# Cosine attention followed by a low-rank mixer and an MLP: mixer tiles that wait in DRAM, another order of the score bursts, and a fifth pair of tiles with seven products in both layers

## The chip, the cores and the metric

The kernel runs on one core of a Trainium2 chip. The metric is the device time of one execution in microseconds; the median of several runs is compared. The engines are TensorE (PE in the profile), VectorE (DVE), ScalarE (ACT), GpSimd (POOL) and SyncE (SP), and 16 DMA engines that serve the queues of POOL and SP.

## The reference, cut to what matters

There are 8 batches, 12 heads, 448 positions and a head width of 64. Each head is normalised, scored, put through a softmax and multiplied with its values. The heads side by side are a matrix of 448 x 768 for each batch. A low-rank map over the positions (rank 32) is added to it, and a two-layer MLP (768 to 3072 to 768) with a residual follows.

```
q_n = q / (norm(q) + 1e-6);  k_n = k / (norm(k) + 1e-6)
attn = softmax(q_n @ k_n.T / tau)
x = heads_side_by_side(attn @ v)                 # 8 x 448 x 768
u = x + (x.transpose(0, 2, 1) @ U @ V).transpose(0, 2, 1)
out = u + relu(u @ w_ch1) @ w_ch2
```

All matmuls of the kernel take bf16 operands and add up in fp32.

## The kernel before, in words

**A program that plans itself.** Each piece of work is an `Op` with an engine, an expected duration, the ops that it depends on (`deps`), the buffers that it takes (`acq`) and gives back (`rel`). Buffers are `Slot`s of a `Ring`; the eight PSUM banks are shared by several `BankRing`s. `Plan.run` goes through time with these durations, gives every engine its next op, and so fixes the order of instructions on each engine. On PE the ops stand in streams with a fixed order of preference: the values of attention (`pe_av`), the mixer (`pe_z0`, `pe_a`), the scores (`pe_sc`) and, last, the MLP (`pe_mlp`), which fills what the others leave. POOL has one stream (`pool_q`) in the order in which the code writes it. ACT, DVE and SP take what is ready by priority. On the chip each engine works through its list in order and waits on semaphores where an input is not there.

**Attention of a batch** (`att`, `scores`, `values`). POOL loads q and k in thirds of four heads, and v. `stats` and `norm` compute the norms on ACT and DVE and scale q and k; SP turns them with DMA transposes into `qkT` (for the first two batches PE does it). A slot of scores is one pair of heads against up to 128 keys: two matmuls of 448 columns, one for each head, which use one half of the rows of the array each. 448 keys make three slots of 128 keys and a rest of 64; the rests of two pairs share a slot of four matmuls that use one quarter of the array each. From batch 2 on `groups_of` puts the three slots of rests of a batch first and then the 18 others, and cuts the list into bursts of three, seven a batch. ACT takes the exp of each slot (L727). `values` (L754) multiplies with v; DVE divides by the sum of the softmax and writes X.

**The mixer** (`stage0`). Two batches (896 positions) make seven tiles of 128 positions, so that tile 3 holds the end of the even batch and the start of the odd one. A is X projected on U; one product with V for each tile and half of the columns, and an add of X on DVE (L918, L920, L923), give the tile u. Tile 3 is made in the odd batch, from both batches' A and X. The tiles u lie in eight SBUF buffers (`r_u`) until the MLP has added its residual.

**The MLP.** There are 28 tiles. The plan's MLP work is done in this order:
- Five plain units (`mlp`) of 3, 4, 3, 3 and 3 tiles. `columns_of` turns their u by DMA transposes into uT (one buffer). The first layer is 24 blocks of six matmuls over all columns of the unit (384 or 512; L1273), each followed by a relu on ACT or DVE. The second is 24 matmuls of 384 columns for each tile and half of the output (L1309), an add of the residual on DVE and stores on SP.
- Two pairs of tiles with seven products in the second layer alone (`mlp_seven` without `up`): the 2 x 2 block product (two tiles by two halves of the output, two halves of the inner width) is made of seven products instead of eight, 84 matmuls of 384 columns (L1196) instead of 96. The first layer is plain, 288 matmuls of 256 columns for both tiles (L1167).
- Four pairs with seven products in both layers (`up_seven`): the first layer is 252 matmuls of 128 columns (L1066).

The seven products need sums of blocks of the weights and of the data. The sums of the second layer's weights are made by `seven_weights`, those of the first by `seven_rows`, which puts them into attention's buffers and therefore waits for the last batch. The sums of the data after the relu are made by `sums_of` (L1148 to L1151): in the pairs with seven products in both layers its last difference is done by POOL for the first two of three groups and by DVE for the third. In each pair, product 1 of the second layer is copied by ACT (L1217), POOL adds u to the copy three times (L1219), and DVE adds the banks of the other products to these (L1212). PE's order there is product 1, 4, 6, 5, 7, 2, 3; the sum that DVE makes after product 6 goes into the bank to which product 7 adds.

**What ties attention to the MLP.** The bursts of batches 2 to 7 have extra dependencies on matmuls of the MLP: batch 2's on the first layer of unit 1, batches 3 to 5's on places in the second layers of units 1 to 3 (`SPOTS`), and batches 6 and 7's on places in unit 4 and in the first two pairs. The first burst of a batch also waits for the mixer's products of the batch before.

Of the kernel before, what the change touches and what calls it, by code (L numbers as in the profile page):

```python
# [101 lines left out]
class Plan:  # L102
# [53 lines left out]
    def run(self):  # L156
# [22 lines left out]
        while left:  # L179
# [6 lines left out]
            while progress:  # L186
                progress = False
                for e in self.ENGINES:
# [81 lines left out]
def kernel(  # L270
# [30 lines left out]
    SPOTS = {8: [(6,)] * 7 + [()], 6: [(5, 17), (10,), (6,), (6,), (6,), (6,)]}  # L301
# [47 lines left out]
    r_u = fixed_ring([u_t[:, i, :] for i in range(8)])  # L349
# [55 lines left out]
    r_low = bank_ring([(5,), (4,), (3,), (2,), (1,), (0,)], 2)  # L405
# [327 lines left out]
    def values(b, p, X):  # L733
# [39 lines left out]
        for hh in range(2):  # L773
# [21 lines left out]
    prev, first_v, made = {}, {}, {}  # L795
# [51 lines left out]
    def stage0(b, X, muls):  # L847
# [39 lines left out]
        us = [Slot(r_u, 2 if b == 0 else 6 if by_pe else 3) for t in tiles]  # L887
# [7 lines left out]
        for z, (c0, c1) in enumerate(cols):  # L895
            for i, t in enumerate(tiles):
# [3 lines left out]
                elif t == 3:  # L900
                    parts = [(prev["A"], PAD + 128 * t), (A, 0)]
# [24 lines left out]
                rel = [mm, X] + ([prev["X"]] if t == 3 else [])  # L926
# [3 lines left out]
                adds[z, i] = plan.add(Op("DVE", dve_t(c1 - c0) * (2 if t == 3 else 1), add,  # L930
# [104 lines left out]
    def up_seven(tiles, relu, tops, ready, left, made_by, x_free):  # L1035
# [61 lines left out]
        for k in (1, 6, 2, 7, 5, 3, 4):  # L1097
            for g in range(len(gs)):
# [25 lines left out]
                else:  # L1124
# [3 lines left out]
                    sums_of(gs[g], relu, ready, [x["r11"]], [x["r12"]], [x["r21"]], [x["r22"]], "POOL" if g < 2 else "DVE")  # L1128
# [26 lines left out]
    def mlp_seven(tiles, right, made_by, up=None, after=()):  # L1155
# [58 lines left out]
        def tile_of(s):  # L1214
# [5 lines left out]
            out=y_.tile, in0=s1.tile, in1=u.tile[:, c0:c0 + CH]), deps=[cp], acq=[y_], rel=[s1, u]), pool_q)  # L1220
            for y_, u, c0 in ((y12, u1, CH), (y22, u2, CH), (y21, u2, 0))]
        if up is not None:
# [13 lines left out]
            x11 = dve(bank(tile_of(o11), lambda: u1.tile[:, 0:CH], a), [p2], [o11], [a, u1])  # L1236
# [8 lines left out]
        x11 = dve(bank(tile_of(o11), lambda: u1.tile[:, 0:CH], a), [p2], [o11], [a, u1])  # L1245
# [14 lines left out]
    def mlp(b, tiles, us, uT, ut):  # L1260
# [42 lines left out]
        for group in groups:  # L1303
# [12 lines left out]
            for (i, t, c0, c1), mm in zip(group, mms):  # L1316
# [5 lines left out]
                    deps=[last[mm]] + got.get((b, "u"), []), acq=[O], rel=[mm, us[i]], prio=1))  # L1322
# [68 lines left out]
    def groups_of(b):  # L1391
# [87 lines left out]
    UNITS = [[(0, 0), (0, 1), (0, 2)], [(0, 3), (0, 4), (0, 5), (0, 6)], [(1, 0), (1, 1), (1, 2)],  # L1479
             [(1, 3), (1, 4), (1, 5)], [(1, 6), (2, 0), (2, 1)]]  # L1480
    for b, tiles in enumerate(UNITS):
        mlp(b, tiles, *(state[b] if b < PE_BATCHES else columns_of(tiles)))
    rest = [(z, t) for z in range(2, 4) for t in range(7)][2:]
    seven = seven_weights(last_down[len(UNITS) - 1],
                          [o for p in range(NPAIR) for o in got[B - 1, p, "qkT"][1]],
                          [last_av[B - 2, p] for p in range(NPAIR)])
    PURE = 4
    hosts = []
    for n in range(0, len(rest), 2):
        if n // 2 == len(rest) // 2 - PURE:  # L1490
            up = seven_rows([hosts[-1][0][-1]], [last_av[B - 1, p] for p in range(NPAIR)])
            held = list(stores)
            up = *up, [o for t in range(7) for o in made[3, t][1]]
        late = n // 2 >= len(rest) // 2 - PURE
        hosts.append(mlp_seven(rest[n:n + 2], *seven, *((up, held) if late else ())))
    (t0, l0), (t1, l1) = hosts[:2]
    t4, d4 = anchors[4]
# [50 lines left out]
```

## Time and profile before

| | us |
|---|---|
| median of 3 runs | 565.98 (565.66 to 566.13) |
| the profiled execution | 565.53 |
| its span, first to last instruction | 563.8 |
| PE busy | 552.9 (98%) |
| DVE busy | 395.4 (70%) |
| ACT busy | 282.1 (50%) |
| POOL busy | 135.2 (24%) |
| SP's DMA queue | 23.98 MB, 21.5% of 16 engines |
| POOL's DMA queue | 25.73 MB, 40.9% of 16 engines |

The span is the time from the first to the last instruction in one profiled execution; some 1.7 us of the execution's time lie around it. The busy time of PE is the union of its matmuls' spans, and these overlap: a matmul of 384 columns is shown with 326 ns, and the next one starts 162 ns after it. What a matmul costs in a stream is the distance from start to start, which is the length of a piece in the chain of waits over its number of matmuls. In the windows by stage each row gives the stretch, its length, then busy time and number of instructions for PE, PE's weight loads, DVE, ACT and POOL, the granted clock of TensorE, the busy share of the DMA engines and what they moved in GB/s. The share can exceed 1[...]. In the timeline a bracket holds the idle time before an instruction and what ended it.

The last score matmuls run at 411 us and the last products with v at 416 us; the four pairs with seven products in both layers fill the time from 445.6 us on.

### The profile page before, as it was taken

The page shows a single profiled execution, that of the slowest core. Times are in us where ns is not written, and L with a number is a line of the kernel's source. Part 1 is how long each engine was busy: PE and PEld are TensorE (multiplying, and loading weights), DVE is VectorE, ACT ScalarE, POOL GpSimd, SP SyncE. Part 2 cuts the span into 40 slices and gives each one's busy share as a digit, 9 for nine tenths or more (in the row PEclk, how much of TensorE's full clock was granted, in tenths as well). Part 3 has the DMA queues.
Part 4 walks back from the last instruction along what each step waited for, and adds up shares of the span by engine and source line. Part 5 has one row for each costly group of instructions (what it writes and reads, how often), then busy time and mean ns, then how long its engine had stood idle before and what let it go on. Part 6 is the DMA issues. An engine that isn't in the chain of part 4 may idle for free.

```text
span 563.8 us, 13573 instructions
## 1 busy us (share of the span) xinstructions
PE 552.9 (98%) x5639; PEld 361.0 (64%) x5639; DVE 395.4 (70%) x901; ACT 282.1 (50%) x466; POOL 135.2 (24%) x170
## 2 busy tenths in 40 slices
PE   8999999999999999999999999999999999999996
PEld 6565566544565565566555655677677787878783
DVE  8989969987674786478337743489468685858582
ACT  7876645668525671666554665336343131414140
POOL 8526242060041105002310300000102013131313
PEclk9899999999999999999999999999999999999999
DMA  9999999795769649596958534310211111112201
GB/s 149 201 208 135 209 199 151 120 111 80 121 77 152 96 68 104 111 114 55 103 107 131 56 30 102 73 29 16 31 44 29 57 30 57 30 57 30 57 3 56
DMA packets 132670, 50.58 MB, mean 90 GB/s; under 512 B 97760, under 2 KB 132608, under 8 KB 132608
## 3 DMA queue, kind: packets, MB, share of 16 engines
q0 software_dynamic: 72352, 25.73, 40.9%
q1 hardware_dynamic: 60256, 23.98, 21.5%
q8 instruction: 44, 0.72, 0.6%
q14 instruction: 18, 0.15, 0.1%
HBM read 52.02 MB, written 11.01 MB: 112 GB/s over the span
## 4 chain that ended last, share of the span: by engine, by line
PE 84%; DVE 9%; issue 2%; POOL 1%; ACT 1%; POOLq 1%; DMA 1%; DVEq 0%
PE bank L1309 23%; PE bank L1273 23%; PE bank L1196 9%; PE bank L754 8%; PE bank L709 6%; PE bank L1167 6%; PE bank L1066 5%; DVE relu L1088 4%; PE bank L909 2%; DVE v_nat L1088 1%; PE bank L502 1%; POOL relu L1151 1%; ACT attn L722 1%; PE bank L859 1%; POOLq L1543 1%
## 5 line engine op out<-in xcount | busy, mean ns | idle before, releaser
L727 ACT ACTIVATE attn<-bank 128x896 bf16<-128x896 f32 (+1 forms) x163 | 139.0, 917 | 72.9 <-PE bank L709 72.4
L1309 PE MATMUL bank<-w_sb,relu 128*128 128x384 bf16 x768 | 136.7, 326 | 0.0
L1273 PE MATMUL bank<-uT,w_sb 128*128 128x384 bf16 (+1 forms) x720 | 135.7, 337 | 0.0
L1309 PEld LDWEIGHTS <-relu 128*128 128x128 bf16 x768 | 70.9, 98 | 52.7 <-issue 10.3
L1273 PEld LDWEIGHTS <-w_sb 128*128 128x128 bf16 x720 | 67.1, 98 | 54.8 <-issue 7.4
L1196 PEld LDWEIGHTS <-relu 128*128 128x128 bf16 x504 | 48.6, 98 | 34.8 <-issue 4.1
L580 DVE TENSOR_REDUCE ss<-sq_all 112x8 f32<-112x512 bf16 x96 | 61.9, 672 | 3.8 <-ACT sq_all L572 3.4
L1296 ACT ACTIVATE relu<-bank 128x384 bf16<-128x384 f32 (+1 forms) x80 | 40.8, 511 | 46.4 <-PE bank L1273 46.0
L648 DVE TENSOR_TENSOR qk_all<-qk_all,inv 112x512 bf16<-112x512 bf16 x93 | 60.7, 680 | 0.1
L754 PEld LDWEIGHTS <-attn 128*128 128x128 bf16 (+1 forms) x1536 | 54.5, 98 | 9.2 <-issue 3.1
L754 PE MATMUL bank<-v_nat,attn 128*128 128x65 bf16 (+1 forms) x1536 | 57.5, 193 | 0.5 <-DVE qkT L1338 0.3
L1196 PE MATMUL bank<-w_sb,relu 128*128 128x384 bf16 x288 | 50.1, 326 | 2.1 <-DVE qkT L1212 1.0
L524 POOL DMA_DIRECT2D qk_all<-in_q_dram x24 | 17.4, 727 | 136.9 <-ACT attn L727 50.2
L547 POOL DMA_DIRECT2D v_nat<-in_v_dram x42 | 31.1, 746 | 72.7 <-PE bank L754 41.7
L709 PE MATMUL bank<-qkT 64*128 64x448 bf16 (+1 forms) x384 | 47.3, 357 | 1.2 <-ACT qkT L1336 0.6
L1320 DVE TENSOR_TENSOR O_sb<-bank,u_nat 128x384 f32<-128x384 f32 x32 | 17.7, 555 | 34.2 <-PE bank L1309 34.0
L785 DVE TENSOR_TENSOR X_sb<-bank,rd 128x256 bf16<-128x256 f32 x96 | 38.9, 416 | 1.6 <-DVE rd L783 0.2
L1151 POOL TENSOR_TENSOR relu<-relu 128x512 bf16<-128x512 bf16 x8 | 17.2, 2170 | 88.2 <-ACT qkT L1217 42.7
L783 DVE RECIPROCAL rd<-bank 128x4 f32<-128x4 f32 x96 | 16.5, 176 | 27.7 <-PE bank L754 26.8
L1298 DVE TENSOR_SCALAR relu<-bank 128x384 bf16<-128x384 f32 (+1 forms) x40 | 23.3, 584 | 16.9 <-PE bank L1273 16.4
L572 ACT ACTIVATE sq_all<-qk_all 112x512 bf16<-112x512 bf16 x53 | 31.1, 630 | 7.6 <-DVE ss L580 7.6
L1066 PE MATMUL bank<-uT,w_sb 128*128 128x128 bf16 x576 | 34.1, 219 | 0.0
(116 smaller groups left out, 643.6 us busy)
## 6 DMA issues: line engine op xcount, KB each, us to landing
qk_all<-in_q_dram POOLq DMA_DIRECT2D x23, 224.0 KB, 5.4
qk_all<-in_k_dram POOLq DMA_DIRECT2D x23, 224.0 KB, 6.3
w_sb<-in_moe_w_ch_dram POOLq DMA_DIRECT2D x4, 1152.0 KB, 18.8
w_sb<-in_moe_w_ch_dram POOLq DMA_DIRECT2D x8, 576.0 KB, 15.8
out_dram<-O_sb SPq DMA_DIRECT2D x13, 168.0 KB, 2.3
v_nat<-in_v_dram POOLq DMA_DIRECT2D x11, 168.0 KB, 8.7
out_dram<-O_sb SPq DMA_DIRECT2D x12, 144.0 KB, 2.8
out_dram<-O_sb SPq DMA_DIRECT2D x12, 120.0 KB, 2.0
```

The lines of the kernel that those rows point to most:

```text
L580: lambda i=i, a0=a0, a1=a1, sq=sq: nc.vector.reduce_sum(ss.tile[:, i, a0:a1, :].rearrange("p h c -> p (h c)"), sq.tile[:, 0:a1 - a0, :].re ...
L648: nc.vector.tensor_mul(dst, src, sc)
L709: nc.tensor.matmul(out=out, lhsT=qkT.tile.rearrange("p b s -> p (b s)")[r, n0:n0 + w], rhs=qkT.tile[r, SC:2 * SC, :].rearrange("p c s -> p ...
L727: exps.append(plan.add(Op("ACT", act_t(2 * S, 0.08), lambda sc=sc, c=c, attn=attn: nc.scalar.activation(out=attn.tile[:, :, off:off + S] i ...
L754: nc.tensor.matmul(out=av.tile[:, t, 0:D + 1], lhsT=tail.tile[:, hh, 128 * t:128 * (t + 1)] if tail and j == SC - 1 else (attn if j < SC - ...
L785: muls.append(plan.add(Op("DVE", dve_t(256), lambda av=av, rd=rd, h=h: nc.vector.tensor_mul(X.tile[:, :, h * D:(h + 1) * D], av.tile[:, :, ...
L1066: o = plan.add(Op("PE", pe_t(128), lambda i=i, j=j, jj=jj: nc.tensor.matmul(out=mm.tile[:, 128 * jj:128 * jj + 128], lhsT=left[k](i, j), r ...
L1167: o = plan.add(Op("PE", pe_t(256), lambda j=j, e=e, cc=cc, mm=mm: nc.tensor.matmul(out=mm.tile[:, 256 * e:256 * e + 256], lhsT=w1_sb[:, cc ...
L1196: o = plan.add(Op("PE", pe_t(CH), lambda j=j: nc.tensor.matmul(out=mm.tile[:, 0:CH], lhsT=left[k](j), rhs=right[k](j), start=(first and j ...
L1273: o = plan.add(Op("PE", pe_t(n), lambda cc=cc: nc.tensor.matmul(out=mm.tile[:, 0:n], lhsT=w1_sb[:, cc, f * 128:(f + 1) * 128], rhs=uT.tile ...
L1296: nc.scalar.activation(out=relu.tile[:, f, 0:n], in_=mm.tile[:, 0:n], func=AF.Relu)
L1309: nc.tensor.matmul(out=mm.tile[:, 0:c1 - c0], lhsT=relu.tile[:, f, i * 128:(i + 1) * 128], rhs=w2_t[:, f, c0:c1], start=(f == 0), stop=(f ...
```

## The change

- **u tiles in DRAM.** For batches 2 to 7 each finished tile u is written by SP into a DRAM tile (`kept`). `columns_of` takes the DMA transposes from there, and reads the tile back into SBUF for the residual (`u.back`). The eight SBUF buffers become two rings of four (`r_us` for making, `r_ur` for the residual).
- **Tile 3** is made in two halves, the first 64 rows in the even batch, the others in the odd one.
- **Score bursts.** The dependencies on the MLP's matmuls go. In batches 3 to 7 burst 0 waits for the last product with v of the batch before, burst 1 for that batch's mixer products, bursts 3 and up for the products with v of pair k - 3 of its own batch.
- **Rests of keys.** The three slots of 64-key rests are spread over the batch (`LAST`): each is sorted to the end of a burst of other slots.
- **Units.** The plain units are of 3, 4, 3 and 4 tiles; two pairs have seven products in the second layer alone, five pairs in both.
- `sums_of` in `up_seven` is on DVE for all three groups. `r_low` may hold four banks. From batch 2 on the first product with v also takes the X buffer. A count of needed buffers in `Plan.run` is corrected.

```diff
@@ Plan.run
-                            room = [x.ring.free_at(new[:n].count(x.ring)) for n, x in enumerate(new)]
+                            room = [x.ring.free_at([y.ring for y in new[:n]].count(x.ring)) for n, x in enumerate(new)]
...
-    SPOTS = {8: [(6,)] * 7 + [()], 6: [(5, 17), (10,), (6,), (6,), (6,), (6,)]}
+    PLAIN = [3, 4, 3, 4]
+    HALF = 2
+    LAST = {0: 0, 2: 2, 4: 4}, {0: 0, 2: 0, 4: 4}
...
-    r_u = fixed_ring([u_t[:, i, :] for i in range(8)])
+    r_us = fixed_ring([u_t[:, i, :] for i in range(4)])
+    r_ur = fixed_ring([u_t[:, i, :] for i in range(4, 8)])
+    dram = ctx.enter_context(tc.tile_pool(name="dram", bufs=1, space=bass.MemoryType.DRAM))
+    kept = {(z, t): dram.tile([128, C], BF, name=f"u_{z}_{t}") for z in range(1, B // 2) for t in range(7)}
...
-    r_low = bank_ring([(5,), (4,), (3,), (2,), (1,), (0,)], 2)
+    r_low = bank_ring([(5,), (4,), (3,), (2,), (1,), (0,)], 4)
@@ values
-                        deps=exps + got[b, h, "v"] + ready if first else (), acq=[av] if first else [],
+                        deps=exps + got[b, h, "v"] + ready if first else (), acq=([av] if b < 2 else [av, X]) if first else [],
@@ columns_of
-            u, adds = made[x]
+            ut.append(plan.add(Op("SP", 0.1, lambda i=i, x=x: nc.sync.dma_start_transpose(
+                out=uT.tile[:, :, i * 128:(i + 1) * 128], in_=kept[x]),
+                deps=[made[x]], acq=[uT.slot], prio=0, lat=("x", 0.05 * 48, 2.0))))
+            u = Slot(r_ur, 2)
+            u.back = plan.add(Op("SP", 0.1, lambda x=x, u=u: nc.sync.dma_start(out=u.tile, in_=kept[x]),
+                                 deps=[made[x]], acq=[u], prio=1, lat=("x", 1.0, 2.0)))
             us.append(u)
-            ut.append(plan.add(Op("SP", 0.1, lambda i=i, u=u: nc.sync.dma_start_transpose(
-                out=uT.tile[:, :, i * 128:(i + 1) * 128], in_=u.tile),
-                deps=adds, acq=[uT.slot], rel=[u], prio=0, lat=("x", 0.05 * 48, 2.0))))
@@ stage0
-        us = [Slot(r_u, 2 if b == 0 else 6 if by_pe else 3) for t in tiles]
+        if not by_pe:
+            tiles = range(4) if par == 0 else range(3, 7)
+        us = [prev["u3"] if b > 1 and b % 2 and t == 3 else
+              Slot(r_ur if b == 1 else r_us, 2 if b == 0 else 6 if by_pe else 1) for t in tiles]
+        if not by_pe:
+            prev["u3"] = us[-1]
...
-                    parts = [(prev["A"], PAD + 128 * t), (A, 0)]
+                    parts = [(prev["A"], PAD + 128 * t), (A, 0)] if by_pe else [(A, 0 if par else PAD + 128 * t)]
...
-                    if t == 3:
+                    if t == 3 and not by_pe:
+                        r = slice(64 * par, 64 * par + 64)
+                        nc.vector.tensor_add(out=u.tile[r, c0:c1], in0=mm.tile[r, 0:w],
+                                             in1=X.tile[r, 3 - 3 * par, c0:c1])
+                    elif t == 3:
...
-                made[b // 2, t] = us[i], [adds[0, i], adds[1, i]]
+                x, u = (b // 2, t), us[i]
+                u_adds[x] = [adds[0, i], adds[1, i]] + u_adds.get(x, [])
+                if t == 3 and par == 0:
+                    continue
+                made[x] = plan.add(Op("SP", 0.1, lambda x=x, u=u: nc.sync.dma_start(out=kept[x], in_=u.tile),
+                                      deps=u_adds[x], rel=[u], prio=0, lat=("x", 1.0, 2.0)))
@@ up_seven
-                    sums_of(gs[g], relu, ready, [x["r11"]], [x["r12"]], [x["r21"]], [x["r22"]], "POOL" if g < 2 else "DVE")
+                    sums_of(gs[g], relu, ready, [x["r11"]], [x["r12"]], [x["r21"]], [x["r22"]], "DVE")
@@ mlp_seven: the residual adds wait for u.back
-            out=y_.tile, in0=s1.tile, in1=u.tile[:, c0:c0 + CH]), deps=[cp], acq=[y_], rel=[s1, u]), pool_q)
+            out=y_.tile, in0=s1.tile, in1=u.tile[:, c0:c0 + CH]), deps=[cp, u.back], acq=[y_], rel=[s1, u]), pool_q)
@@ mlp
-        todo = bursts.get(b + 2, ()) if 0 < b < 4 else ()
-        for o, f in zip(bursts.get(2, ()) if b == 1 else (), [0,3,6,9,12,15,18,21]):
-            o.deps.append(tops[f])
-        spots = [(g, f) for g in range(len(downs)) for f in SPOTS[len(downs)][g]] if todo else ()
-        for o, (g, f) in zip(todo, spots):
-            o.deps.append(downs[g][f])
@@ groups_of
-        slots = [(p, SC - 1) for p in range(0, NPAIR, 2)] if b >= TB else []
+        slots = []
         for p in range(NPAIR):
+            if b >= TB:
+                slots += [(x, SC - 1) for x, at in LAST[b > TB].items() if at == p]
@@ att
-            scores(b, x, first_v.get(b - 1, ()) if n == 0 and b in (2, 3, 4, 5, 6, 7) else ())
+            scores(b, x, first_v.get(b - 1, ()) if n == 0 and b == 2 else ())
@@ the MLP's units and the bursts' dependencies
-    UNITS = [[(0, 0), (0, 1), (0, 2)], [(0, 3), (0, 4), (0, 5), (0, 6)], [(1, 0), (1, 1), (1, 2)],
-             [(1, 3), (1, 4), (1, 5)], [(1, 6), (2, 0), (2, 1)]]
+    every = [(z, t) for z in range(B // 2) for t in range(7)]
...
-    PURE = 4
...
-        if n // 2 == len(rest) // 2 - PURE:
+        if n // 2 == HALF:
...
-    for o, at in zip(bursts[B - 2] + bursts[B - 1], [
-            t4[3], t4[10], t4[17], d4[0][0], d4[1][0], d4[2][0], d4[3][0],
-            d4[4][0], d4[5][0], t0[2], t0[7], l0[0], l0[3], l0[5]]):
-        o.deps.append(at)
+    for b in range(3, B):
+        for k, o in enumerate(bursts[b]):
+            o.deps += ([last_av[b - 1, NPAIR - 1]] if k == 0 else first_v[b - 1] if k == 1 else
+                       [last_av[b, k - 3]] if k > 2 else [])
```

More of the change, by code (lines that the diff above doesn't have):

```diff
@@ L790, in values @@
         return muls
[L795 removed]
+    prev, first_v, made, u_adds = {}, {}, {}, {}
     class Columns:
@@ L925, in stage0 @@
                 first_v.setdefault(b, []).append(o)
-                rel = [mm, X] + ([prev["X"]] if t == 3 else [])
+                rel = [mm, X] + ([prev["X"]] if t == 3 and by_pe else [])
                 for s_ in rel[1:]:
@@ L929, in stage0 @@
                     s_.left += 1
-                adds[z, i] = plan.add(Op("DVE", dve_t(c1 - c0) * (2 if t == 3 else 1), add,
+                adds[z, i] = plan.add(Op("DVE", dve_t(c1 - c0) * (2 if t == 3 and by_pe else 1), add,
                                          deps=[o], rel=rel, prio=0 if b == 1 else 2))
@@ L1235, in mlp_seven @@
             p2 = product(2, a, False, True, [cp])
-            x11 = dve(bank(tile_of(o11), lambda: u1.tile[:, 0:CH], a), [p2], [o11], [a, u1])
+            x11 = dve(bank(tile_of(o11), lambda: u1.tile[:, 0:CH], a), [p2, u1.back], [o11], [a, u1])
             store(tiles[0], 0, CH, o11, x11)
@@ L1244, in mlp_seven @@
         p2 = product(2, a, False, True, [cp])
-        x11 = dve(bank(tile_of(o11), lambda: u1.tile[:, 0:CH], a), [p2], [o11], [a, u1])
+        x11 = dve(bank(tile_of(o11), lambda: u1.tile[:, 0:CH], a), [p2, u1.back], [o11], [a, u1])
         store(tiles[0], 0, CH, o11, x11)
@@ L1321, in mlp @@
                                          in1=us[i].tile[:, c0:c1]),
-                    deps=[last[mm]] + got.get((b, "u"), []), acq=[O], rel=[mm, us[i]], prio=1))
+                    deps=[last[mm], getattr(us[i], "back", None)] + got.get((b, "u"), []), acq=[O], rel=[mm, us[i]], prio=1))
                 store(t, c0, c1, O, o)
@@ L1478 @@
     plan.safe = .2
-    UNITS = [[(0, 0), (0, 1), (0, 2)], [(0, 3), (0, 4), (0, 5), (0, 6)], [(1, 0), (1, 1), (1, 2)],
-             [(1, 3), (1, 4), (1, 5)], [(1, 6), (2, 0), (2, 1)]]
-    for b, tiles in enumerate(UNITS):
+    every = [(z, t) for z in range(B // 2) for t in range(7)]
+    n = 0
+    for b, w in enumerate(PLAIN):
+        tiles = every[n:n + w]
+        n += w
         mlp(b, tiles, *(state[b] if b < PE_BATCHES else columns_of(tiles)))
-    rest = [(z, t) for z in range(2, 4) for t in range(7)][2:]
-    seven = seven_weights(last_down[len(UNITS) - 1],
+    rest = every[n:]
+    seven = seven_weights(last_down[len(PLAIN) - 1],
                           [o for p in range(NPAIR) for o in got[B - 1, p, "qkT"][1]],
                           [last_av[B - 2, p] for p in range(NPAIR)])
-    PURE = 4
     hosts = []
     for n in range(0, len(rest), 2):
-        if n // 2 == len(rest) // 2 - PURE:
+        if n // 2 == HALF:
             up = seven_rows([hosts[-1][0][-1]], [last_av[B - 1, p] for p in range(NPAIR)])
             held = list(stores)
[L1493 to L1497, printed above, removed]
-    for o, at in zip(bursts[B - 2] + bursts[B - 1], [
-            t4[3], t4[10], t4[17], d4[0][0], d4[1][0], d4[2][0], d4[3][0],
-            d4[4][0], d4[5][0], t0[2], t0[7], l0[0], l0[3], l0[5]]):
-        o.deps.append(at)
+            up = *up, [o for t in range(7) for o in u_adds[3, t]]
+        hosts.append(mlp_seven(rest[n:n + 2], *seven, *((up, held) if n // 2 >= HALF else ())))
+    for b in range(3, B):
+        for k, o in enumerate(bursts[b]):
+            o.deps += ([last_av[b - 1, NPAIR - 1]] if k == 0 else first_v[b - 1] if k == 1 else
+                       [last_av[b, k - 3]] if k > 2 else [])
     order = plan.run()
```

## The prediction

> **What bounds the kernel now.** I read the busy row of the page first, then the windows by stage, the chain of waits, and the timeline of one late stage. The windows (span; busy us and count of an engine) say where TensorE has no work:
>
> ```profile
> 0.00:40.00 40.00, 35.62 (x479) 24.86 (x480) 34.65 (x101) 32.30 (x59) 23.45 (x34) 0.96 1.31 184
> 105.30:391.00 285.70, 285.70 (x2643) 169.14 (x2642) 189.45 (x428) 162.14 (x263) 54.32 (x78) 1.00 0.68 89
> 474.10:502.50 28.40, 27.88 (x340) 22.28 (x338) 19.55 (x39) 7.81 (x13) 7.02 (x5) 1.00 0.17 43
> ```
>
> PE is the first pair after the span, DVE the third. From 105 to 391 us PE has no idle time and the granted clock is 1.00; DVE fills 66% of it, the DMA share is 0.68. So a transfer, or ACT or DVE, can't set the end there: PE's work does. What this stretch costs is counted in matmuls. The chain gives their step from start to start:
>
> ```profile
> 62.55 0.97 PE bank L754 x32
> 105.35 17.27 PE bank L1273 x80
> 425.11 6.33 PE bank L1167 x58
> 431.44 7.47 PE bank L1196 x46
> 474.14 6.71 PE bank L1066 x120
> ```
>
> 17.27/80 = 0.2159 us at 512 columns, 7.47/46 = 0.1624 at 384, 6.33/58 = 0.1091 at 256, 6.71/120 = 0.0559 at 128. One place is left where PE waits, once in each of the four last pairs of tiles:
>
> ```profile
> 462.31 4.30 POOL L1151 TENSOR_TENSOR relu<-relu 128x512 bf16<-128x512 bf16 x2 [24.08 <-DVE relu L1149]
> 466.58 0.91 POOL L1219 TENSOR_TENSOR relu<-relu,u_nat 128x384 f32<-128x384 f32 x1
> 467.52 0.56 DVE L1212 TENSOR_TENSOR relu<-bank,relu 128x384 f32<-128x384 f32 x1 [3.03 <-POOL relu L1219]
> 468.13 6.01 PE L1196 MATMUL bank<-w_sb,relu 128*128 128x384 bf16 x36 [0.53 <-DVE relu L1212]
> ```
>
> POOL does two block sums (L1151), then the first residual add (L1219); DVE's sum waits for that add, and PE's product 7 for the sum. The reader should see that the 4.30 us on POOL is what is late.
>
> **The two layers (main part).** 16 plain tiles become 14, four pairs with seven products in both layers become five, two half pairs stay. Matmuls by the code, times the steps above:
> - Before: first layer 576 x 0.1624 + 144 x 0.2159 + 288 x 0.1091 + 1008 x 0.0559 = 93.5 + 31.1 + 31.4 + 56.3; second 768 x 0.1624 + 504 x 0.1624 = 124.7 + 81.8. Sum 419.0 us.
> - After (units of 3, 4, 3, 4): 288 x 0.1624 + 288 x 0.2159 + 288 x 0.1091 + 1260 x 0.0559 = 46.8 + 62.2 + 31.4 + 70.4; 672 x 0.1624 + 588 x 0.1624 = 109.1 + 95.5. Sum 415.4 us.
>
> That is **-3.5 us** (418.97 and 415.42 before rounding). A rule of the Trainium skill speaks against cutting work into small matmuls: "TensorEngine Tiling (Array Packing)", Instruction Overhead, gives each matmul some 60 cycles of overhead. The change has 96 matmuls more (3384 for 3288); at 60 cycles of a 2.4 GHz clock (25 ns) apiece they would take back 2.4 us and leave -1.1. The rows decide: 384 columns more cost 0.2159 - 0.0559 = 0.160 us, so 128 columns cost 0.0533 of the 0.0559, and the overhead is 0.0026 us. It is in the sum already.
>
> **The block sums.** L1151 goes from POOL (2.17 us for 128x512) to DVE (0.416 us for the same shape). POOL's first add then starts after ACT's copy at 462.35 and ends near 463.3; DVE's sum waits for product 6 (459.64 + 36 x 0.1624 = 465.5) and is done by 466.1, before product 7 at 459.64 + 48 x 0.1624 = 467.4. A pair of this kind costs 252 x 0.0559 + 84 x 0.1624 = 27.73 us of PE and takes 28.40, so 4 x 0.67 = **-2.7 us**, and the fifth pair doesn't wait either. DVE gets 0.83 us more in 27.7: 20.4, covered. Were DVE late at product 7 instead, each pair would lose up to the 0.67 again.
>
> **The 64-key slots.** Before, the three of a batch are one burst of their own; now each stands last in a burst of 128-key slots: three such bursts in batch 2, two in each of five later batches, 13 in all (groups_of, counted by hand). Batch 1 has both kinds in the trace:
>
> ```profile
> 66.32 0.55 PE L709 MATMUL bank<-qkT 64*128 64x448 bf16 x4
> 66.80 2.94 PE L1273 MATMUL bank<-uT,w_sb 128*128 128x384 bf16 x17
> 69.67 0.68 PE L709 MATMUL bank<-qkT 64*128 64x448 bf16 x6
> 70.28 0.82 PE L1273 MATMUL bank<-uT,w_sb 128*128 128x384 bf16 x4
> ```
>
> Two slots of one kind take 66.80 - 66.32 = 0.48 us to the next matmul, one of each kind 70.28 - 69.67 = 0.61. The same page (Key Properties) says that a change of tiling mode drains TensorE: a rule against this edit, and the row gives it a price, about 0.12 us. 13 x 0.12 = **+1.5 us**; without the rule I would have put nothing here. The number of bursts (seven a batch) stays.
>
> **The order of attention.** Bursts no longer wait for the MLP's matmuls but for attention's, and u tiles no longer hold SBUF until an MLP unit takes them, so attention runs ahead. It can't go faster than DVE's share of it: per batch 61.9/8 (sums of squares) + 60.7/8 (norms) + (38.9 + 16.5)/8 + u adds 25.5/6 + some 5 for squares, roots and copies = 29 to 30 us, where a batch now takes 52. At 33 us a batch it ends near 305 us instead of 416. PE's total is the same: 14 us a batch of attention, the rest filled with MLP. **0 us**, hidden while MLP work is ready; uncovered, each us that PE waits for an exp costs one. The densest stretch of now has bursts 4.0 to 4.4 us apart (122 to 137, 277 to 291 us) and no PE idle. The first value product of a batch now waits for an X buffer too; behind it stand only that batch's values, and X has two buffers, freed by the u adds of two batches before. The product for t=3 is split: one half moves to the even batch, with 16 such matmuls a pair of batches before and after and as many adds.
>
> **The scratch.** Per waiting tile SP issues one write (196 KB) and one read back more, 42 DMAs; the 21 transposes read DRAM. Stores issue in 0.42 us on SP: 18 us more over 450. Queued behind a waiting write on SP are qkT transposes, uT transposes and output stores; the scores wait for the first. A transpose from SBUF lands in 2.8 us. From DRAM no row shows it: between that and, with write (2.1, as the stores) and double the time, 8 us. Further down, POOL's residual adds wait for the read back, with the next adds queued behind them, and DVE's sum for those. I take nothing: a read back asked for at a pair's start has 14 us (252 x 0.0559) of first layer to land, uT is free when a first layer ends, and 13.6 us (84 x 0.1624) of second layer, or more, follow. Two landings later than 13 us would show as PE idle at a first layer.
>
> **Sum.** -3.5 - 2.7 + 1.5 = -4.7. The profiled execution is 565.53 (span 563.8, 1.7 around it), so 560.8; the median of the runs is 565.98, 0.45 above: **561.3 us**. PE's start (4.4 us of gaps before 40 us) and the 4.4 us after the last matmul stay.
>
> **Rivals.**
> - *Dense attention costs PE a little.* Bursts reserve six of eight banks, so a 512-column first layer has two banks, and a late relu holds PE. For: two four-tile units now. Against: 122 to 137 us is such a stretch without idle. At 0.3 us for each of some ten chunks, 3 us: 564.3.
> - *POOL's stall only changes place* (DVE late at product 7): five pairs keep 28.40, 561.3 + 5 x 0.67 = 564.6.
> - *Slower: the loads set the pace.* PE's order is fixed, so a late q, k or v lets PE stand. DMA work from 105 to 391 us is 0.68 x 286 = 194 us; the scratch adds 42 x 0.197 = 8.3 MB, by the mean of SP's queue (21.5% of 563.8 us for 23.98 MB) 42 us. That is 236 us for six batches in 200: a share near 1.2. Against: the first 40 us ran at 1.31, and q and k have a batch of lead (three load buffers, six of qkT). If the queues gave only 1.05, as at 214 to 246 us, the six batches would need 225 us, 4 us more each; with half of it hidden by the buffers 12 us of waiting: 573. It decides from 4.7 us of waiting, under 1 us a batch.
> - *The change does less harm than I count:* bursts that touch each other save the 0.18 us of entry and exit (in the timeline 0.258 us from a 384-column matmul to a burst where its step is 0.162, and 0.282 after the last slot where slots follow at 0.19); a dozen of them 2 us: 559.2.
>
> **Numbers.** Likeliest (559.8 to 562.6) 0.62; touching bursts 0.08; dense 0.16; POOL 0.06; loads 0.06; the rest small. Within 0.2% (1.1 us, about what these runs tell from no change) of 565.98 ends at 564.9; a bad case of dense or POOL falls there. Faster 0.90, same 0.04, slower 0.06. The range 559.0 to 564.6 leaves out the loads, the worst dense cases and a little below; the likeliest alone is 559.8 to 562.6.
>
> **What would show it.** Pairs of the last kind at 27.7 us with no [<-DVE] before product 7; L1066 x1260, L1273 x576; mixed bursts 0.12 us longer; last L754 before 330 us; PE busy equal to its window from 40 us on. Idle on PE at L709 or L754 would prove me wrong by the loads, at L1273 by banks.

## The result, and the profile after

The changed kernel takes **562.0 us** (median of 4 runs, 560.98 to 562.06) where the kernel before takes 566.06 beside it (565.66 to 566.33): a ratio of 0.9925, interval 0.9908 to 0.9942. The profiled execution takes 560.98 us with a span of 559.2, against 565.53 and 563.8. In a second comparison the same kernel gave 561.32 (0.9913, 0.99 to 0.9927).

The page of the changed kernel: busy time by engine, SP's DMA queue (packets, MB, share of 16 engines), and two of SP's DMA issues (median us from issue to landing at the end).

```profile
PE 550.2 (98%) x5735; PEld 359.8 (64%) x5735; DVE 412.1 (74%) x940; ACT 281.9 (50%) x461; POOL 132.2 (24%) x165
...
q1 hardware_dynamic: 66304, 32.25, 26.5%
...
u<-u_nat SPq DMA_DIRECT2D x21, 192.0 KB, 2.3
u_nat<-u SPq DMA_DIRECT2D x21, 192.0 KB, 2.9
```

DVE has 17 us more work, SP's queue 8.3 MB more. A tile is written in 2.3 us and read back in 2.9; a transpose from DRAM lands in 3.5 (2.8 from SBUF before), by the view of the transfers:

```profile
uT<-u SPq DMA_TRANSPOSE x21, 3.5
```

The windows of the changed kernel, in the columns of those before (stretch, length, then PE, weight loads, DVE, ACT, POOL, the granted clock, DMA share, GB/s), with one of the last pairs of tiles at the end:

```profile
0.00:40.00 40.00, 35.30 (x477) 24.69 (x478) 34.50 (x101) 32.12 (x58) 23.25 (x34) 0.96 1.31 185
105.30:391.00 285.70, 285.70 (x2765) 165.69 (x2764) 205.49 (x472) 166.93 (x263) 56.94 (x81) 1.00 0.77 113
471.73:499.45 27.72, 27.72 (x339) 22.29 (x337) 20.23 (x41) 7.81 (x13) 5.17 (x3) 1.00 0.22 57
```

PE is still busy all through the middle, with the DMA share up from 0.68 to 0.77 and the clock at 1.00. The last pair has no gap either: 27.72 us, all of it matmuls, where it was 28.40 with 27.88 busy. The chain of waits shows the same pairs from the first one on (start, length, engine and line, matmuls):

```profile
402.64 13.65 PE bank L1217 x84
416.29 14.07 PE bank L1087 x252
430.36 13.65 PE bank L1217 x84
444.01 14.07 PE bank L1087 x252
```

The pieces join without a rest: 402.64 + 13.65 = 416.29, and so on. Their steps are those of before, 13.65/84 = 0.1625 us and 14.07/252 = 0.0558.

**Where the time went**, from the starts of the matmuls in the two profiled executions. The first four rows add up to the fifth; a wait is what a start-to-start distance holds beyond the usual one.

| | before | after | difference |
|---|---|---|---|
| the first MLP matmul starts | 38.03 | 38.30 | +0.27 |
| 53 score bursts, to the next matmul | 33.83 | 35.33 | +1.50 |
| all other matmuls | 484.42 | 480.93 | -3.49 |
| waits of PE after 40 us | 2.74 | 0.0 | -2.74 |
| the last matmul starts | 559.02 | 554.56 | -4.46 |

The last matmul ends at 559.35 and 554.89 us, and the tail after it is 4.4 and 4.3 us. The three terms of the prediction's sum (-3.5, -2.7, +1.5) stand in the table as -3.49, -2.74 and +1.50.

### The profile page after: what moved, and what is told of

It is laid out like the page before. It is cut to its first block, busy times and chain, and to the rows that moved or that the text cites. A ratio compares the mean times of both kernels' runs of the same rounds, so it can differ in the third digit from the quotient of the medians.

```text
span 559.2 us, 13870 instructions
## 1 busy us (share of the span) xinstructions
PE 550.2 (98%) x5735; PEld 359.8 (64%) x5735; DVE 412.1 (74%) x940; ACT 281.9 (50%) x461; POOL 132.2 (24%) x165
## 4 chain that ended last, share of the span: by engine, by line
PE 94%; DVE 3%; ACT 1%; DMA 1%; issue 0%; DVEq 0%
PE bank L1330 20%; PE bank L1294 20%; PE bank L1217 17%; PE bank L1087 13%; PE bank L759 8%; PE bank L714 7%; PE bank L1188 6%; PE bank L921 2%; PE bank L507 1%; DVE qk_all L653 1%; ACT attn L727 1%; PE bank L866 1%; DVE ss L585 1%; DMA relu<-in_q_dram 1%; DVE X_sb L790 0%
## 5 line engine op out<-in xcount | busy, mean ns | idle before, releaser
L1330 PE MATMUL bank<-w_sb,relu 128*128 128x384 bf16 x672 | 121.0, 326 | 0.0
L1294 PE MATMUL bank<-uT,w_sb 128*128 128x384 bf16 (+1 forms) x576 | 119.8, 353 | 0.0
L1294 PEld LDWEIGHTS <-w_sb 128*128 128x128 bf16 x576 | 52.9, 98 | 51.9 <-issue 8.7
L1217 PE MATMUL bank<-w_sb,relu 128*128 128x384 bf16 x336 | 58.1, 326 | 0.0
L714 PE MATMUL bank<-qkT 64*128 64x448 bf16 (+1 forms) x384 | 48.8, 359 | 1.1 <-ACT attn L727 0.6
L1317 ACT ACTIVATE relu<-bank 128x512 bf16<-128x512 f32 (+1 forms) x59 | 32.1, 545 | 32.4 <-PE bank L1294 32.2
L1087 PE MATMUL bank<-uT,w_sb 128*128 128x128 bf16 x720 | 42.6, 219 | 0.0
L1087 PEld LDWEIGHTS <-w_sb 128*128 128x128 bf16 x720 | 41.0, 98 | 0.6
L1124 ACT COPY X_sb<-bank 128x512 f32<-128x512 f32 x15 | 8.8, 587 | 60.4 <-PE bank L1087 59.5
L1240 POOL TENSOR_TENSOR relu<-relu,u_nat 128x384 f32<-128x384 f32 x3 | 5.0, 1663 | 129.8 <-ACT relu L1238 129.8
```

Source lines behind the costliest of these rows:

```text
L714: nc.tensor.matmul(out=out, lhsT=qkT.tile.rearrange("p b s -> p (b s)")[r, n0:n0 + w], rhs=qkT.tile[r, SC:2 * SC, :].rearrange("p c s -> p ...
L1087: o = plan.add(Op("PE", pe_t(128), lambda i=i, j=j, jj=jj: nc.tensor.matmul(out=mm.tile[:, 128 * jj:128 * jj + 128], lhsT=left[k](i, j), r ...
L1217: o = plan.add(Op("PE", pe_t(CH), lambda j=j: nc.tensor.matmul(out=mm.tile[:, 0:CH], lhsT=left[k](j), rhs=right[k](j), start=(first and j ...
L1294: o = plan.add(Op("PE", pe_t(n), lambda cc=cc: nc.tensor.matmul(out=mm.tile[:, 0:n], lhsT=w1_sb[:, cc, f * 128:(f + 1) * 128], rhs=uT.tile ...
L1317: nc.scalar.activation(out=relu.tile[:, f, 0:n], in_=mm.tile[:, 0:n], func=AF.Relu)
L1330: nc.tensor.matmul(out=mm.tile[:, 0:c1 - c0], lhsT=relu.tile[:, f, i * 128:(i + 1) * 128], rhs=w2_t[:, f, c0:c1], start=(f == 0), stop=(f ...
```

## The experiments

Each line edited is small, but the plan is made anew with it, so other instructions can move too; where they did, the text says so. "Waits" are those of PE after 40 us in the profiled execution, counted as in the table above.

| run | median us | ratio to before, interval | waits of PE, us |
|---|---|---|---|
| after_again: the changed kernel | 561.32 | 0.9913, 0.99 to 0.9927 | 0 |
| a_pool: block sums back on POOL | 564.90 | 0.9976, 0.9967 to 0.9986 | 3.4 |
| b_dve: before, block sums on DVE | 563.39 | 0.995, 0.9938 to 0.9962 | 0 |
| a_mix: one more plain unit, one pair fewer | 564.61 | 0.9973, 0.9964 to 0.9982 | 0 |
| a_rests: 64-key slots in one burst | 564.58 | 0.9982, 0.9973 to 0.9992 | 4.7 |
| b_spread: before, 64-key slots spread | 569.38 | 1.0064, 1.0052 to 1.0076 | 4.2 |
| a_notie: no ties of the bursts | 567.58 | 1.0026, 1.0014 to 1.0038 | 4.4 |
| a_half1: a sixth pair, nothing else | 567.71 | 1.0028, 1.0017 to 1.004 | 5.9 |
| a_margin: smaller margin in the plan | 562.18 | 0.9933, 0.9921 to 0.9946 | 1.2 |
| a_six: margin and sixth pair | 559.60 | 0.9885, 0.987 to 0.99 | 0.6 |
| a_six_banks: and more banks | 562.10 | 0.9934, 0.9921 to 0.9946 | 1.5 |
| a_write4: four writes of each tile | 561.33 | 0.992, 0.9906 to 0.9933 | 0.3 |

### The block sums: one edit, undone and done alone

a_pool:

```diff
-                    sums_of(gs[g], ..., [x["r22"]], "DVE")
+                    sums_of(gs[g], ..., [x["r22"]], "POOL" if g < 2 else "DVE")
```

b_dve is the opposite edit in the kernel before. With them the changed kernel ran again.

> The changed kernel as it is, beside the others of this call as their standard. All theories: 561.5 to 562.2 us, 0.9915 to 0.9935 of the kernel before.

> The changed kernel with the last block difference of two groups of three back on POOL. Theory (POOL's 4.3 us ahead of its first residual add stall product 7 by 0.67 us a pair, as in the four pairs of before): five pairs at 28.40 instead of 27.73 us, so 3.4 us more than the changed kernel, about 565.4. Rival (DVE is the busier engine, and what POOL gives back DVE loses elsewhere): the same as the changed kernel, 562.0.

> The kernel before with that difference on DVE for all three groups, nothing else. Theory: four pairs at 27.73 instead of 28.40 us, 2.7 us less, about 563.4. Rival (DVE comes late to the sum before product 7 and the wait stays): 566.1.

Undone, the edit costs 564.90 - 561.32 = 3.6 us; done alone it brings 566.16 - 563.39 = 2.8, against four times 0.67 = 2.7 worked out beforehand. The timeline of a_pool, in one of its five pairs (start, length, engine, line; the idle time before it and what ended it in the bracket):

```profile
490.21 4.30 POOL L1172 TENSOR_TENSOR relu<-relu 128x512 bf16<-128x512 bf16 x2 [21.38 <-ACT relu L1238]
494.47 2.76 POOL L1240 TENSOR_TENSOR O_sb<-relu,u_nat 128x384 f32<-128x384 f32 x3
495.41 0.56 DVE L1233 TENSOR_TENSOR O_sb<-bank,O_sb 128x384 f32<-128x384 f32 x1 [3.03 <-POOL O_sb L1240]
496.02 6.01 PE L1217 MATMUL bank<-w_sb,relu 128*128 128x384 bf16 x36 [0.52 <-DVE O_sb L1233]
```

It is the stall of before: 4.30 us of sums on POOL, then the add, then DVE's sum, then product 7. All five pairs have it, 3.4 us together. With the sums on DVE none of the pairs waits, in either kernel. The rival that the stall only changes its place falls.

### The two layers

a_mix takes back the number of plain units and pairs; attention's order, its ties and the scratch stay.

```diff
-    PLAIN = [3, 4, 3, 4]
+    PLAIN = [3, 4, 3, 3, 3]
```

> The changed kernel with 16 plain tiles (3, 4, 3, 3, 3), two half pairs and four pairs with seven products in both layers, as before; all else as changed. Theory: 3.5 us of matmuls more than the changed kernel, about 565.5. Rival (the fifth pair costs elsewhere what it saves in matmuls): 562 to 563.

564.61 is 3.3 us above after_again and 2.6 above the first comparison; the profiled execution takes 564.46, 3.5 more than that of the changed kernel, with no wait of PE and 484.4 us of other matmuls, the number of before. So the -3.5 is the count of matmuls at their steps, as worked out.

### The 64-key slots: both ways

a_rests puts the three slots of rests of a batch together again:

```diff
-    LAST = {0: 0, 2: 2, 4: 4}, {0: 0, 2: 0, 4: 4}
+    LAST = {0: 0, 2: 0, 4: 0}, {0: 0, 2: 0, 4: 0}
```

> The changed kernel with the three slots of 64-key rests of a batch in one burst of their own again, ahead of the others. Theory of the prediction (a change of array mode inside a burst costs 0.12 us, 13 times, and nothing else hangs on the spread): 1.5 us less than the changed kernel, about 560.5. Rival (a burst of rests completes no pair, so ACT spends three exps and PE the six banks before the first product with v can start, and tied to attention's own products the whole batch comes later: batch's end moves back by some us each and PE waits where MLP work can't fill): some us more, 565 to 567, with idle time on PE before scores or products with v.

b_spread brings the spread alone to the kernel before:

```diff
-        slots = [(p, SC - 1) for p in range(0, NPAIR, 2)] if b >= TB else []
+        slots = []
+        LAST = {0: 0, 2: 2, 4: 4}, {0: 0, 2: 0, 4: 4}
         for p in range(NPAIR):
+            if b >= TB:
+                slots += [(x, SC - 1) for x, at in LAST[b > TB].items() if at == p]
```

> The kernel before with the 64-key rests spread as in the change (three mixed bursts in batch 2, two in each of the five later batches), nothing else; bursts stay tied to the MLP's matmuls. Theory: 13 changes of array mode at 0.12 us, 1.5 us more than before, about 567.6. Rival (the change of mode hides behind what the burst waits for anyway): 566.1.

The price of the switch is as it was read from batch 1. Timeline of the changed kernel, two bursts of three slots, the first with a 64-key slot (8 matmuls), the second without (6):

```profile
362.49 0.86 PE L714 MATMUL bank<-qkT 64*128 64x448 bf16 x8
363.29 0.94 PE L1188 MATMUL bank<-uT,w_sb 128*128 128x256 bf16 x7
...
373.34 0.74 PE L714 MATMUL bank<-qkT 64*128 64x448 bf16 x6
374.02 0.66 PE L1217 MATMUL bank<-w_sb,relu 128*128 128x384 bf16 x3
```

To the next matmul it is 363.29 - 362.49 = 0.80 us and 374.02 - 373.34 = 0.68: 0.12 for the switch. Over all bursts the spread adds 1.50 us in the changed kernel and 1.48 in b_spread.

But a_rests, which saves this 1.5, is slower by 3.3 us. PE waits 4.7 us in it: 3.2 at bursts, the rest at products with v, at a product of the mixer and at two products of a pair's second layer. Timeline of a_rests at two of the three bursts that wait:

```profile
184.82 0.74 PE L714 MATMUL bank<-qkT 64*128 64x448 bf16 x6
186.22 0.65 PE L759 MATMUL bank<-v_nat,attn 128*128 128x65 bf16 x16 [0.66 <-ACT attn L732]
...
367.42 0.57 PE L714 MATMUL bank<-qkT 64*128 64x448 bf16 x3
369.02 0.54 PE L714 MATMUL bank<-qkT 64*128 64x448 bf16 x3 [1.02 <-DVE X_sb L790]
```

The first is followed by values that have to wait for its own exps; the second stops in its middle until DVE has written X. All three are bursts of 128-key slots (6 matmuls). The six bursts of 64-key slots don't wait: each takes 0.69 us to the next matmul, as in the kernel before. In a_rests the last products with v also come at 391 us, not 379. 4.7 less the 1.5 of switches makes 3.2 us; the profiled execution is 3.5 longer than that of the changed kernel. So what was costed as a pure price did not come alone: with the slots bunched the plan of the whole of attention comes out later and PE waits in other places. Whether the bunching itself or only the new plan does that is open; the two can't be told apart with one plan each.

b_spread is 3.3 us slower than before, not 1.5. 1.4 us of the rest are new waits in batch 2 (timeline of b_spread):

```profile
131.38 0.63 ACT L572 ACTIVATE sq_all<-qk_all 112x512 bf16<-112x512 bf16 x1 [2.01 <-DMA qk_all<-in_q_dram]
131.91 0.58 ACT L1296 ACTIVATE relu<-bank 128x512 bf16<-128x512 f32 x1
132.54 1.02 PE L1273 MATMUL bank<-uT,w_sb 128*128 128x512 bf16 x4 [0.31 <-ACT relu L1296]
...
134.01 0.65 PE L754 MATMUL bank<-v_nat,attn 128*128 128x65 bf16 x16 [0.45 <-ACT attn L727]
```

A load of q came late, a square on ACT waited 2.01 us for it, and a relu and the exps stood behind that square. (The four stalls at product 7, 2.74 us, are in the table's 4.2 as before.) With the 1.48 of switches that is the 2.9 by which its profiled execution (568.42) is longer than that of before. Its median is 569.38; what the other runs lose beyond the profiled one is not known.

### The order of attention: without the ties

In a_notie the bursts of batches 3 to 7 are tied neither to the MLP nor to attention:

```diff
-    for b in range(3, B):
+    for b in range(3, 3):
```

> The changed kernel without any dependency of a burst of batches 3 to 7 on attention's products or on the mixer's. Theory of the prediction (where PE is full of MLP work the order of attention costs nothing): 562.0, within 0.5. Rival (the ties keep bursts from taking six banks early, before their exps' buffers and the mixer's products have had theirs, and without them PE stands between bursts): 4 to 7 us more, 566 to 569, with idle time on PE.

567.58, 6 us slower. Timeline and windows (PE's busy time alone, clock, DMA share, GB/s) of a_notie:

```profile
190.83 0.73 PE L714 MATMUL bank<-qkT 64*128 64x448 bf16 x2
192.46 0.57 PE L714 MATMUL bank<-qkT 64*64 64x448 bf16 x8 [0.90 <-DVE u_nat L931]
...
195.12 0.65 PE L759 MATMUL bank<-v_nat,attn 128*128 128x65 bf16 x16 [2.09 <-ACT attn L732]
```

```profile
190.00:195.00 5.00, 2.11 (x31) 1.00 0.72 152
195.00:200.00 5.00, 4.72 (x46) 0.66 0.01 2
```

Bursts pile up: scores wait until DVE's adds of u free a bank, values wait for their exps, and after that the granted clock is 0.66. The bursts take 3.67 us more than in the changed kernel and all else of PE 2.18 more, which, less 0.13 at the start, is the 5.7 between the profiled executions (566.67 and 560.98). 4.4 us of it are waits, and some 1.5 are matmuls at a slower clock. "0 us" holds with the ties alone.

A batch takes 42.1 us in a_notie (the last products with v start at 369.2 us), against 45.4 in the changed kernel. So the ties set 3 us of a batch's length, and no more.

### A sixth pair, and what lets it in

If attention ended as early as forecast, the next pair could have seven products in both layers too: it would take 27.72 us instead of 144 x 0.1091 + 84 x 0.1624 = 29.35, which is 1.6 less. a_half1 is this edit:

```diff
-    HALF = 2
+    HALF = 1
```

> The changed kernel with one half pair and six pairs with seven products in both layers. By the count alone: first layer of one pair 252 x 0.0559 instead of 144 x 2 x 0.1091 us, 15.7 - 14.1, so 1.6 us less: 560.4. Rival (attention ends at 379 us and the sixth pair would start near 388; the sums of the first layer's weights take twelve DVE passes of 0.95 us, 11 us, after the last product with v, so its products wait): 3 to 6 us more, 565 to 568, with PE idle before the first matmuls of 128 columns.

567.71, 6 us slower. Timeline and windows (columns as above) of a_half1:

```profile
386.50 2.17 PE L1087 MATMUL bank<-uT,w_sb 128*128 128x128 bf16 x36
...
391.92 0.23 PE L1087 MATMUL bank<-uT,attn 128*128 128x128 bf16 x1 [3.19 <-DVE attn L1047]
...
394.53 1.78 PE L1087 MATMUL bank<-uT,attn 128*128 128x128 bf16 x15 [2.38 <-DVE attn L1047]
```

```profile
388.00:392.00 4.00, 0.81 (x15) 1.00 0.44 148
392.00:396.00 4.00, 1.62 (x16) 0.73 0.00 0
396.00:400.00 4.00, 4.00 (x64) 0.85 0.01 4
400.00:404.00 4.00, 4.00 (x75) 1.00 0.23 49
```

The sums of the first layer's weights (L1047, `seven_rows`) go into attention's buffers, which the last batch still holds at 379 us, and keep DVE at work from then on; PE waits for these sums twice, up to 391.92 and up to 394.53.

Two theories remained for attention's pace: it is bound by DVE and the loads, or it is a chain of bursts in which each link carries a margin of the plan (PE's instructions are placed `plan.safe` after their inputs are expected). a_margin cuts the margin of batches 2 to 7:

```diff
-        plan.safe = .2 if b == 1 else .5
+        plan.safe = .2 if b == 1 else .3
```

a_six is a_margin with `HALF = 1`. a_six_banks has `HALF = 1`, a margin of 0.25, and `r_av3`, the values' ring of PSUM banks, may hold four banks in place of two.

> The changed kernel with the plan's margin ahead of each PE op of batches 2 to 7 cut from 0.5 to 0.3 us, so that attention's chain (burst, three exps, products with v, DVE, next burst) is planned closer. Theory (the length of this chain with its margins, not DVE's work, sets the 46 us of a batch; the end is set by PE's work, which stays): a batch takes some 43 to 44 us, the last product with v comes near 367 instead of 379 us, and the time is that of the changed kernel, 561.7 within 0.6. Rival 1 (DVE or the loads set the pace): the last product with v stays near 379 us. Rival 2 (the margin was needed): PE waits for exps, 2 us or more slower.

> The same margin of 0.3 us, and one half pair with six pairs that have seven products in both layers. Theory (what the sixth pair lacked was the early end of attention): with the last product with v near 367 us the weight sums are ready when the sixth pair starts near 387, so the count holds: 1.6 us less than the changed kernel, about 560.1, with no wait of a 128-column matmul for DVE. Rival (DVE has no room for the sums beside attention's end, or margins cost PE): 562 or more.

> As the last one with a margin of 0.25 us, and four instead of two PSUM banks at once for the products with v. Theory (banks held by products with v are a link of the chain that sets a batch's length): the last product with v near 351 us, time 559.5 to 560.5. Rival (closer planning makes PE wait for a late exp or load on the chip): slower than the one before, with idle time on PE at L759 or L714.

The last products with v start at 378.9 us in the changed kernel, 367.9 in a_margin, 366.6 in a_six, 352.4 in a_six_banks; a batch takes 45.4 us in the first, 43.9 in the second and 42.0 in the last. So the margins are links of the chain, and DVE and the loads don't set its 45.4 us (margin and banks changed together in a_six_banks, so what the banks do isn't separate). What holds a batch at 42 us, in a_six_banks as in a_notie, no run shows. By itself the earlier end brings nothing: a_margin's 562.18 is level with the 562.0 and 561.32 of the changed kernel. In a_six the sixth pair fits. The chain of waits of a_six:

```profile
374.09 13.32 PE bank L1217 x82
387.42 14.07 PE bank L1087 x252
```

The first layer of the sixth pair runs its 252 matmuls in 14.07 us, without the wait of a_half1. **559.60 us (559.05 to 560.02), ratio 0.9885, beats both kernels.** Taking the margin and banks further gives it back: a_six_banks takes 562.10. Its profiled execution (561.09) waits 1.5 us; the longest wait, 0.8 us at 133.7, is a first layer's for a relu that stands on DVE behind work on a late load of q.

### The scratch

a_write4 writes each waiting tile to three more DRAM tensors before it counts as written:

```diff
+                def put(x=x, u=u):
+                    for to in (kept, *more):
+                        nc.sync.dma_start(out=to[x], in_=u.tile)
```

> The changed kernel with each waiting tile written to DRAM four times (to three other tensors as well, which nobody reads): 63 more writes, 12.4 MB more on SP's queue, the order of all engines the same. Theory of the prediction (the scratch is hidden): the same as the changed kernel, 561.7 within 0.7. Rival (DMA is close to its limit beside attention, or SP's list holds back the transposes to qkT): 2 us or more slower, with PE idle at scores.

The page (SP's queue, DMA issues) and the windows of a_write4:

```profile
q1 hardware_dynamic: 75376, 44.64, 32.7%
...
m<-u_nat SPq DMA_DIRECT2D x63, 192.0 KB, 2.7
```

```profile
105.00:391.00 286.00, 285.83 (x2762) 165.32 (x2760) 205.35 (x473) 166.74 (x263) 56.80 (x81) 1.00 0.87 148
```

12.4 MB and 63 issues on SP more, a DMA share of 0.87 where it was 0.77, and 561.33 us: no difference from 561.32 (ratios 0.992 and 0.9913). PE has work in 285.83 of 286 us. The scratch is hidden with room left, and at this pace of attention the rival by which the loads set the time falls.

## Why the prediction was right, and where it was not

It gave 561.3 us and 559.0 to 564.6; measured were 562.0 and 561.32.

**The two layers, -3.5: right.** -3.49 in the accounting, 3.5 between profiled executions in a_mix. The row of 0.0559 us for 128 columns held with 1260 of them. The 60 cycles a matmul that were weighed against it (25 ns, which is the time of 60 columns at 0.160 us for 384) would have left -1.1.

**The block sums, -2.7: right in mechanism and size.** 2.74 in the trace, 2.8 in b_dve; five stalls and 3.6 in a_pool. One statement of this step failed: that POOL's first add "ends near 463.3", which is 0.95 us after ACT's copy ends. The timeline of the changed kernel, in the same place, in the first of the five pairs:

```profile
432.42 0.48 ACT L1238 COPY relu<-bank 128x384 f32<-128x384 f32 x1 [0.67 <-PE bank L1217]
...
432.98 3.17 POOL L1240 TENSOR_TENSOR relu<-relu,u_nat 128x384 f32<-128x384 f32 x1 [24.36 <-ACT relu L1238]
...
434.62 0.75 DVE L1172 TENSOR_TENSOR relu<-relu 128x512 bf16<-128x512 bf16 x2
...
436.30 0.56 DVE L1233 TENSOR_TENSOR relu<-bank,relu 128x384 f32<-128x384 f32 x1 [0.92 <-POOL relu L1240]
...
437.99 2.28 PE L1217 MATMUL bank<-w_sb,relu 128*128 128x384 bf16 x13
```

The add takes 3.17 us, not 0.91, and the profile puts 0.92 us of DVE's waiting down to it. It costs nothing, because the sum needs product 6 as well: product 5, which follows product 6, starts at 437.99 - 12 x 0.1624 = 436.04, only 0.1 us before the add ends. The sum is done at 436.86, 1.1 us before product 7. The prediction has this cover in its working, with 2.2 us from the end of the add to that of product 6 (463.3 to 465.5); the add, 2.3 us longer than counted, used them up.

**The 64-key slots, +1.5: the price was right, that nothing else hangs on the spread was not.** The working counted switches and no effect on the order. The switches cost 1.50 (0.12 each, as the row of batch 1 gave; that this time is a drain of TensorE, as the rule cited there has it, the trace doesn't show). What the step left out is that with the slots bunched the new order holds 4.7 us of waits (a_rests), so that taking the spread back doesn't win 1.5 us but loses 3.3. The forecast doesn't suffer from it, since the changed kernel has the spread and no wait; that this spread goes without waits was not worked out beforehand.

**The order of attention, 0 us: right as a sum, wrong in its reasons.** "At 33 us a batch it ends near 305 us" failed: 45.4 us a batch, last products with v at 379 us, so the sign "last L754 before 330 us" was missed. The estimate added up DVE's work in a batch as if DVE were the next bound (its terms make 31.5 us, not the "29 to 30" that stands there). What delays a batch is a chain from burst to burst. Timeline of the changed kernel in batch 4:

```profile
213.81 0.74 PE L714 MATMUL bank<-qkT 64*128 64x448 bf16 x6
214.53 1.72 ACT L732 ACTIVATE attn<-bank 128x896 bf16<-128x896 f32 x2
...
216.12 1.14 PE L759 MATMUL bank<-v_nat,attn 128*128 128x65 bf16 x32
216.53 0.90 ACT L732 ACTIVATE attn<-bank 128x896 bf16<-128x896 f32 x1
217.39 0.73 DVE L790 TENSOR_TENSOR X_sb<-bank,rd 128x256 bf16<-128x256 f32 x2
```

The round is scores, exps, products with v, X and the next burst at 219.1, 5.3 us after the last; there are seven bursts a batch and a longer step between batches. Of the 12 us a batch by which the forecast was short the ties make 3 (a_notie) and the margins 1.5 (a_margin); the rest stays open. The 0 held since PE had MLP work between the links, and the last batch was over 37 us before the first pair with seven products in both layers (416 us), where the forecast had 110. That 37 us are enough was not worked out beforehand. a_half1, with 8 us, shows what a shorter lead does: 6 us. And without the ties, as a_notie shows, the 0 is 6 us as well. The order is thus not worth 0 in every sense: before, attention ended at 416 us, where the fifth pair now starts, so the -3.5 of the layers probably needs it. No run has the fifth pair with the old order.

**The scratch, 0: right.** No first layer waits; the transposes' 3.5 us lies near the lower end of the 2.8 to 8.

**The rivals.** Dense attention: in the changed kernel the bursts of a batch stand mostly 5 to 6 us apart, and no first layer waits. Where bursts come closer (a_notie, a_six_banks), first layers do wait, 0.3 and 0.8 us, but the long waits of a_notie are at scores and values. The loads: no wait here, but a late load of q is behind 1.4 us in b_spread and 0.8 in a_six_banks. The saving of bursts that touch is not in the accounting: all 53 together took 1.50 us more, the switches' price.

## What to carry to other kernels

Where one engine is busy from end to end, count its instructions at their measured start-to-start distance: that gave all three terms within 0.1 us. A step booked as 0 because "other work covers it" needs the place and the size of that cover written down; here the time hung on 1.1 us ahead of product 7, on 37 us ahead of the first pair and on the ties, and using up the second or undoing the third cost 6 us each. In a pipeline whose order is fixed ahead, the sum of each engine's work was a poor forecast of its pace: follow one round of the chain, margins and buffers included.

## What the runs showed of the hardware that was not expected

**A shared port.** POOL's first residual add took 3.17 to 3.25 us in every pair of the changed kernel that has seven products in both layers (0.91 in such pairs of the kernel before and of a_pool), and it ended 0.77 us after the row of DVE's two-input sums that ran beside it: in 5 of 5 pairs here, 4 of 4 in b_dve, 6 of 6 in a_six. In the lines above the sums from 434.62 end at 435.37 and the add at 436.15. Six of the sums beside it began after the add had, each some 0.08 us before the sum ahead of it ended. The Trainium skill ("SBUF — State Buffer", Who interferes with whom) states that a DVE instruction with two SBUF inputs contends with a GpSimd instruction that reads SBUF, and that the port pair which they share is an exclusive lock; the traces agree, at 2.3 us for an add of 0.91. Work moved from POOL to DVE can thus slow what is left on POOL.

**A stall costs more than its length.** In a_half1 the two waits hold 5.9 us with the gaps around them; less 1.6 saved by the count that makes 4.3, and the profiled execution is 5.5 longer. The rest is about what the matmuls lose that run at a slower clock then, 1.3 us: from 394.5 to 397.9 us those of 128 columns start 107 ns apart where it was 56, in windows with a granted clock of 0.73 and 0.85. In a_notie, after 5 us in which PE was busy for 2.11, those of 384 columns start 320 ns apart where it is 162, until 199.7 us, though no single wait was longer than 2.1 us. "TensorE: Matmul & The Clock Gate" (What's actually happening) puts the fall to half the clock after an idle window of about 3.4 us; the first run fits that, and in the second less idle in one piece was enough.
